# Gram products issued in bursts of their own, and the next chunk's v.r products moved ahead of the state and y products

## The chip, the core and the metric

The kernel runs on one core of one Trainium2 chip. TensorE multiplies into PSUM, ScalarE (ACT) and VectorE (DVE) copy from there to SBUF, GpSimd (POOL) works on SBUF alone, and SP issues most of the transfers. The metric is the device time of one execution in microseconds.

## What is computed

A recurrence over 768 time steps for 4 batches of 8 heads, whose output goes through a routed two-layer network.

```python
for t in range(S):
    y[:, :, t] = np.einsum('bhd,bhde->bhe', rt, state)
    Sa = np.einsum('bhde,bhe->bhd', state, at)
    state_decay = state * wt[:, :, None, :] - np.einsum('bhd,bhe->bhde', Sa, bt)
    state = state_decay + np.einsum('bhd,bhe->bhde', vt, kt)
...
expert_idx = np.argmax(x @ w_gate, axis=1)
h = np.maximum(x_sorted[lo:hi] @ w1[e], 0.0)
y_sorted[lo:hi] = h @ w2[e]
return gate_w[:, None] * y
```

All inputs are f32; S is 768, D is 40, there are 3072 tokens of width 320 and 8 experts with 1024 hidden columns.

## The kernel before, in words

The 768 steps are cut into 12 chunks of 64. A chunk is worked on as two units, each of two batches: 8 groups times 2 halves of the partitions (`HD`), so a product over a unit is 16 matmuls, each of which the trace counts as two passes. The recurrence inside a chunk is turned into matrix products.

For each chunk there are two kinds of work. The *systems* of the next chunk do not need the state: `grams` (products of a and k, b with the decays; the left operand has 128 columns, so these use tiles of another shape than the 64-column products), five `level` products that invert a triangular matrix by halves, `couple` and `whole`. The *rest* of the present chunk needs the state: `right` (ps_q, the right-hand side, first from the state, then from v), `solve` (ps_uT), `zgram` (ps_z), `y_state` and `y_rest` (ps_y), `state` (ps_s), `turned` (ps_S), and `emit` (ps_x), which writes the output rows and gate logits of the chunk before. `atv` (ps_atv, the v.r products) belongs to the next chunk and needs only its inputs.

TensorE, ScalarE and VectorE run in the order in which the code issues their work, and `weave` writes that order: it takes the system pieces of both units by turns (16 pieces a chunk) and puts the matmuls of the rest beside them, two by two, 19 per piece; what doesn't fit beside a piece's 16 matmuls follows it. Items of `rest` that stand in a tuple use all 128 rows of the array; they are not put beside a piece but run as a burst after it, to the end of all such items in a row. `ahead` holds VectorE and GpSimd work (`decay`) for the chunk after next.

A piece's `end` issues the copies out of PSUM. For `grams` these are, per bank pair half, one VectorE multiply (pair, L304) and three ScalarE copies (off L314, nkb L315, GT L316). `parted` is a ScalarE copy of one element (seen, L229) that stands between two products into one bank which use different rows of the array, and TensorE waits for it. PSUM is shared out in two tags with two buffers of two banks each: "sys" for the systems (a unit's Gram products take both) and "rest".

SP issues the loads of the chunk after next in program order; each waits until its buffer's reader is done.

The matmul helper `mm` is line 222, so nearly all of TensorE's rows carry L222 and are told apart by their tiles.

Of the kernel before, what the change touches and what calls it, by code (L numbers as in the profile page):

```python
# [8 lines left out]
F32 = mybir.dt.float32  # L9
# [12 lines left out]
def kernel(  # L22
# [96 lines left out]
    with tc.tile_pool(name="ring", bufs=1) as ring, \  # L119
# [198 lines left out]
            return ts, end  # L318

        def stack(name, s, w):  # L320
            return [sb.tile([128, G, w], F32, name=f"{name}{s}_{par}") for par in range(2)]

        def atv(u):

# [167 lines left out]
        def y_state(us):  # L492
            for u, ps in zip(us, banks("ps_y", T2)):
                c, s = u
                d = units[u]
                d["py"] = ps
                if c:
                    yield [lambda g=g, par=par: mm(
                        ps[own(par), g, :], s_r[s][0][oth(par, D), g, :], d["ri"][oth(par, D), g, :T2],
                        start=(g == 0), stop=False, free=True) for g, par in HD], lambda ps=ps: parted(ps)  # L500

        def y_rest(us):
            for u in us:
                c, s = u
                d = units[u]
                ps = d["py"]

                def end():
                    t = d["y"] = sb.tile([128, G, T2], F32, name="y", bufs=4)
                    nc.scalar.copy(t[:], ps[:])  # L510
                    nc.gpsimd.tensor_tensor(t[:], t[:], d["PT"][:, :, :T2], op=ALU.mult)
                yield [lambda g=g, par=par: mm(
                    ps[own(par), g, :], d["nkb"][par][:, g, :], d["az"][par][:, g, :],
                    start=(c == 0), free=True) for g, par in HD], end
# [22 lines left out]


        def weave(systems, rest, count, ahead, lead=0):
            def flow():  # L540
                for it in rest:
                    alone = isinstance(it, tuple)
                    for ts, end in (it[0] if alone else [it()] if callable(it) else it):
                        for i, t in enumerate(ts):
                            yield t, (end if i == len(ts) - 1 else None), alone

            f = flow()
            kept = []

            def run(n, beside=False):  # L550

                while n > 0:
                    t, end, alone = kept.pop() if kept else next(f, (None, None, None))
                    if t is None:
                        return 0
                    if alone and beside:
                        kept.append((t, end, alone))
                        return n
                    t()
                    if end:  # L560
                        end()
                    n -= 1
                    if alone and n <= 0:
                        n = 1
                        t = next(f, None)
                        if t is not None:
                            kept.append(t)
                        if t is None or not t[2]:
                            n = 0
                return 0  # L570

            ahead = list(ahead)
            per = -(-count // max(len(systems), 1))
            for n, piece in enumerate(systems):
                ts, end = piece()
                left = per
                for i in range(0, len(ts), 2):
                    for t in ts[i : i + 2]:
                        t()
                    left -= min(2, left) - run(min(2, left), True)  # L580
                end()
                run(left)
                if n >= lead and ahead:
                    ahead.pop(0)()
            for a in ahead:
                a()
            run(10 ** 6)

        def chain(u):
            return ([lambda: grams(u)] + [lambda k=k: level(u, k) for k in range(5)]  # L590
                    + [lambda: couple(u), lambda: whole(u)])

        def systems(us):
# [2 lines left out]
        def rest(us, nx, before):  # L596
            last = us[0][0] + 1 == NS
            ps = [right(us), solve(us)] + [lambda u=u: zgram(u) for u in us]
            ps += [y_state(us), (emit(before),)] if before else [y_state(us)]
            if not last:  # L600
                ps += [(state(us),)]
            ps += [(y_rest(us),)] + [lambda u=u: atv(u) for u in nx]
            if not last:
                ps += [turned(us)]
            return ps

        with tc.manual_schedule(engines={mybir.EngineType.PE, mybir.EngineType.DVE, mybir.EngineType.Activation}):
# [21 lines left out]
            def with_fill(piece, n):  # L629
                def f():  # L630
                    ts, end = piece()

                    def end_():
                        end()
                        for _ in range(n):
                            if fill:
                                fill.pop(0)()
                    return ts, end_
                return f
            one[:3] = [with_fill(one[0], 2), with_fill(one[1], 2), with_fill(one[2], 1)]  # L640

            def late(u):
                return [lambda i=i: decay(u)[i]() for i in range(5)]
# [275 lines left out]
```

## Time and profile before

| | us |
|---|---|
| median of 2 runs | 1236.79 (1234.4 to 1239.18) |
| the profiled execution | 1237.3 |
| its span, first to last instruction | 1235.5 |
| TensorE busy in matmuls | 1031.9 (84% of the span) |
| VectorE, ScalarE, GpSimd busy | 365.1, 340.1, 363.0 |
| Gram products (ps_gram), 768 passes | 144.8 |
| level products (ps_lv), 3840 passes | 244.1 |

A busy row of TensorE is not TensorE at its peak: matmuls are pipelined, and one row's duration overlaps the next. How long a stretch takes is read from the starts of its rows in the timeline. The granted clock stands in the windows as a share of 2.4 GHz.

### The profile page before, as it was taken

The numbers are of one execution on the slowest core, as the hardware profiler recorded it, in microseconds if no ns is written. First come the engines' busy times: TensorE is split into PE (matmuls) and PEld (weight loads), VectorE is DVE, ScalarE is ACT, GpSimd is POOL, SyncE is SP. The second block draws the span as 40 slices with busy tenths as digits, with TensorE's granted clock in tenths as the row PEclk, the third lists the DMA queues.
The fourth block names the chain that finished last, engine by engine and source line by source line (L and its number), as shares of the span: only waits on it lengthen the run. The fifth ranks groups of instructions, "written<-read, shape, count | busy, mean of one in ns | idle before, by whom it ended". The sixth has DMA issues, their size and how long they took to land. (4 is left out here: it accounts for less than half of the span.)

```text
span 1235.5 us, 32075 instructions
## 1 busy us (share of the span) xinstructions
PE 1031.9 (84%) x14204; PEld 770.7 (62%) x14204; DVE 365.1 (30%) x681; ACT 340.1 (28%) x732; POOL 363.0 (29%) x393
## 2 busy tenths in 40 slices
PE   1788879788787878787887888785599999999996
PEld 1667768676777767686867777685244554455444
DVE  2623452433414252524424252303311011011100
ACT  0324342433323343424334233432001111011110
POOL 8434342422423243423323342212501211220001
PEclk9966776666757676666667576765599999999998
DMA  3121221111202121111112010003612322231100
GB/s 85 43 46 31 48 48 26 38 36 33 45 22 46 28 51 23 41 32 34 40 32 46 2 24 12 13 3 74 183 54 89 102 79 94 75 121 59 45 16 17
DMA packets 119584, 59.82 MB, mean 48 GB/s; under 512 B 103825, under 2 KB 115091, under 8 KB 119444
## 3 DMA queue, kind: packets, MB, share of 16 engines
q1 hardware_dynamic: 109156, 47.55, 15.0%
q0 software_dynamic: 3072, 9.20, 2.4%
q8 instruction: 113, 1.85, 0.6%
q10 hardware_dynamic: 7216, 1.00, 0.5%
q14 instruction: 27, 0.22, 0.1%
HBM read 49.83 MB, written 9.19 MB: 48 GB/s over the span
## 5 line engine op out<-in xcount | busy, mean ns | idle before, releaser
L222 PE MATMUL ps_lv<-pair,N 64*64 64x96 f32 (+2 forms) x3840 | 244.1, 270 | 43.1 <-DVE pair L373 21.0
L222 PEld LDWEIGHTS ps_lv<-pair,N 64*64 64x64 f32 x3840 | 208.5, 161 | 51.8 <-ACT GT L316 21.8
L823 PE MATMUL hp<-xgT,w 128*128 128x512 f32 (+1 forms) x384 | 192.3, 631 | 0.0
L222 PE MATMUL ps_gram<-ai,kb 40*128 40x104 f32 x768 | 144.8, 441 | 42.1 <-POOL ai L275 24.7
L836 PE MATMUL zp<-w,h_sb 128*128 128x320 f32 x512 | 145.0, 433 | 0.0
L347 DVE STREAM_TRANSPOSE N<-pair 128x512 f32<-128x512 f32 x120 | 83.8, 699 | 193.7 <-ACT pair L370 192.9
L823 PEld LDWEIGHTS hp<-xgT,w 128*128 128x128 f32 (+1 forms) x384 | 63.3, 189 | 123.7 <-issue 122.6
L222 PEld LDWEIGHTS ps_gram<-ai,kb 40*128 40x128 f32 x768 | 97.2, 283 | 61.4 <-POOL ai L275 24.7
L836 PEld LDWEIGHTS zp<-w,h_sb 128*128 128x128 f32 x512 | 94.6, 191 | 34.5 <-issue 0.8
L842 POOL DMA_INDIRECT out_dram<-zo,s_idx x32 | 31.8, 992 | 279.1 <-ACT zo L841 251.2
L304 DVE TENSOR_TENSOR pair<-ps_gram,nup 64x512 f32<-64x512 f32 x48 | 33.1, 689 | 268.6 <-PE ps_gram L222 267.8
L284 POOL TENSOR_TENSOR kb<-kb,wi 128x512 f32<-128x512 f32 x48 | 61.0, 1270 | 118.6 <-DVE wi L281 104.5
L828 DVE TENSOR_SCALAR h_sb<-hp 128x512 f32<-128x512 f32 x32 | 22.1, 692 | 247.5 <-PE hp L823 247.5
L281 DVE RECIPROCAL wi<-PT 128x128 f32<-128x128 f32 x96 | 88.3, 925 | 0.1
L310 POOL TENSOR_TENSOR pair<-pair 128x256 f32<-128x256 f32 x24 | 17.4, 724 | 238.3 <-DVE pair L304 238.3
L830 ACT ACTIVATE h_sb<-hp 128x512 f32<-128x512 f32 x32 | 19.1, 597 | 202.1 <-PE hp L823 196.9
L370 ACT COPY pair<-ps_lv 128x512 f32<-128x512 f32 x96 | 56.1, 584 | 63.2 <-PE ps_lv L222 51.0
L222 PE MATMUL ps_q<-st,ai 40*64 40x40 f32 x704 | 69.9, 291 | 3.3 <-ACT seen L229 3.3
L222 PE MATMUL ps_atv<-ri,v 40*64 40x104 f32 x768 | 71.6, 286 | 0.0
L462 POOL TENSOR_TENSOR az<-az,up 128x512 f32<-128x512 f32 x48 | 59.5, 1271 | 30.2 <-ACT az L461 30.1
L222 PEld LDWEIGHTS ps_q<-st,ai 40*64 40x64 f32 x704 | 47.1, 181 | 29.5 <-issue 20.8
L222 PE MATMUL ps_q<-vu,GT 64*64 64x40 f32 x768 | 55.6, 305 | 7.9 <-ACT q L431 4.6
(163 smaller groups left out, 1434.6 us busy)
## 6 DMA issues: line engine op xcount, KB each, us to landing
w<-in_moe_w_dram SPq DMA_DIRECT2D x8, 1280.0 KB
w<-in_moe_w_dram SPq DMA_DIRECT2D x8, 1024.0 KB
kb<-in_packed_dram SPq DMA_DIRECT2D x176, 40.0 KB
v<-in_packed_dram SPq DMA_DIRECT2D x96, 40.0 KB
wp<-in_packed_dram SPq DMA_DIRECT2D x96, 40.0 KB
ri<-in_packed_dram SPq DMA_DIRECT2D x96, 40.0 KB
x_rows<-xr SPq DMA_DIRECT2D x48, 80.0 KB
a<-in_packed_dram SPq DMA_DIRECT2D x88, 40.0 KB
```

The source lines that it names most:

```text
L222: nc.tensor.matmul(out_, lhsT=lhs, rhs=rhs, start=start, stop=stop, skip_group_check=free)
L281: nc.vector.reciprocal(wi[:, h, p : p + 2], by_batch(d["PT"][:, :, 1:])[:, h, p : p + 2])
L284: nc.gpsimd.tensor_tensor(kb, kb, wi[:, h, :, None, :].to_broadcast([128, NP, 2, T2]), op=ALU.mult)
L304: nc.vector.tensor_tensor(parts(nt)[own(par)], ps[own(par), :, :T2].rearrange("q g (a t) -> q g a t", a=2), nup[own(par)].rearrange("q (a ...
L347: nc.vector.transpose(N[:].rearrange("q g a t -> q a g t"), nt)
L370: nc.scalar.copy(parts(new[:, :2]), ps[:, :, :T2].rearrange("q g (a t) -> q g a t", a=2))
L462: nc.gpsimd.tensor_tensor(t[:], t[:], up64[:, None, :].to_broadcast([128, G, T2]), op=ALU.mult)
L823: nc.tensor.matmul(hp[:, :cols], lhsT=g["w"][0][:dsz, db, fb * 128 : (fb + 1) * 128], rhs=g["xT"][:dsz, db, :cols], start=(db == 0), stop= ...
L828: nc.vector.tensor_relu(g["h"][:, fb, :cols], hp[:, :cols])
L830: nc.scalar.activation(g["h"][:, fb, :cols], hp[:, :cols], AF.Relu)
L836: nc.tensor.matmul(zp[:], lhsT=g["h"][:, fb, j * 128 : (j + 1) * 128], rhs=g["w"][1][:, fb, :], start=(fb == 0), stop=(fb == FB - 1),)
L842: ins_ = nc.gpsimd.indirect_dma_start(out=out[:, :], out_offset=bass.IndirectOffsetOnAxis(ap=g["si"](j), axis=0), in_=zo[:], in_offset=Non ...
```

## The change

Gram pieces are marked in a list, `alone`, and `weave` puts nothing beside them; the 19 matmuls of the rest that belong to such a piece follow its end. The flag that was called `alone` is now `full`. In `rest`, `emit` moves from behind `y_state` to its front and out of the burst with `state` and `y_rest`, the `atv` products come next, and `y_state` moves from ahead of `emit` to behind `state`. So that `atv` can write while the present chunk's vu and az are still read, `stack` gets two buffers.

```diff
@@ -318,7 +318,7 @@
             return ts, end
 
         def stack(name, s, w):
-            return [sb.tile([128, G, w], F32, name=f"{name}{s}_{par}") for par in range(2)]
+            return [sb.tile([128, G, w], F32, name=f"{name}{s}_{par}", bufs=2) for par in range(2)]
 
         def atv(u):
 
@@ -539,10 +539,10 @@
         def weave(systems, rest, count, ahead, lead=0):
             def flow():
                 for it in rest:
-                    alone = isinstance(it, tuple)
-                    for ts, end in (it[0] if alone else [it()] if callable(it) else it):
+                    full = isinstance(it, tuple)
+                    for ts, end in (it[0] if full else [it()] if callable(it) else it):
                         for i, t in enumerate(ts):
-                            yield t, (end if i == len(ts) - 1 else None), alone
+                            yield t, (end if i == len(ts) - 1 else None), full
 
             f = flow()
             kept = []
@@ -550,17 +550,17 @@
             def run(n, beside=False):
 
                 while n > 0:
-                    t, end, alone = kept.pop() if kept else next(f, (None, None, None))
+                    t, end, full = kept.pop() if kept else next(f, (None, None, None))
                     if t is None:
                         return 0
-                    if alone and beside:
-                        kept.append((t, end, alone))
+                    if full and beside:
+                        kept.append((t, end, full))
                         return n
                     t()
                     if end:
                         end()
                     n -= 1
-                    if alone and n <= 0:
+                    if full and n <= 0:
                         n = 1
                         t = next(f, None)
                         if t is not None:
@@ -577,7 +577,8 @@
                 for i in range(0, len(ts), 2):
                     for t in ts[i : i + 2]:
                         t()
-                    left -= min(2, left) - run(min(2, left), True)
+                    if piece not in alone:
+                        left -= min(2, left) - run(min(2, left), True)
                 end()
                 run(left)
                 if n >= lead and ahead:
@@ -586,8 +587,12 @@
                 a()
             run(10 ** 6)
 
+        alone = []
+
         def chain(u):
-            return ([lambda: grams(u)] + [lambda k=k: level(u, k) for k in range(5)]
+            first_piece = lambda: grams(u)
+            alone.append(first_piece)
+            return ([first_piece] + [lambda k=k: level(u, k) for k in range(5)]
                     + [lambda: couple(u), lambda: whole(u)])
 
         def systems(us):
@@ -596,10 +601,12 @@
         def rest(us, nx, before):
             last = us[0][0] + 1 == NS
             ps = [right(us), solve(us)] + [lambda u=u: zgram(u) for u in us]
-            ps += [y_state(us), (emit(before),)] if before else [y_state(us)]
+            if before:
+                ps += [(emit(before),)]
+            ps += [lambda u=u: atv(u) for u in nx]
             if not last:
                 ps += [(state(us),)]
-            ps += [(y_rest(us),)] + [lambda u=u: atv(u) for u in nx]
+            ps += [y_state(us), (y_rest(us),)]
             if not last:
                 ps += [turned(us)]
             return ps
@@ -637,7 +644,8 @@
                                 fill.pop(0)()
                     return ts, end_
                 return f
-            one[:3] = [with_fill(one[0], 2), with_fill(one[1], 2), with_fill(one[2], 1)]
+            alone.append(with_fill(one[0], 2))
+            one[:3] = [alone[-1], with_fill(one[1], 2), with_fill(one[2], 1)]
 
             def late(u):
                 return [lambda i=i: decay(u)[i]() for i in range(5)]
```

On TensorE, at the turn from the first unit's Gram products (ai_1_108) to the second's (ai_1_110), before:

```order
L222 MATMUL ps_gram<-ai_1_108,kb_1_102 128x104 x2
L222 MATMUL ps_q<-st_0_127,ai_0_107 64x40 x2
L222 MATMUL ps_q<-st_0_128,ai_0_109 64x40 x3
L222 MATMUL ps_gram<-ai_1_110,kb_1_104 128x104 x2
L222 MATMUL ps_q<-st_0_128,ai_0_109 64x40 x2
```

and in the changed kernel, from the last product of the chunk before up to the first ps_q product that reads GT:

```order
L222 MATMUL ps_f<-TT_2187,xt_0_118 64x64 x16
L222 MATMUL ps_gram<-ai_1_108,kb_1_102 128x104 x16
L222 MATMUL ps_q<-st_0_127,ai_0_107 64x40 x16
L222 MATMUL ps_q<-st_0_128,ai_0_109 64x40 x3
L222 MATMUL ps_gram<-ai_1_110,kb_1_104 128x104 x16
L222 MATMUL ps_q<-st_0_128,ai_0_109 64x40 x13
L222 MATMUL ps_q<-vu_0_1923,GT_1541 64x40
L222 MATMUL ps_q<-vu_1_1924,GT_1541 64x40
```

The 16 Gram products of a unit stand together, and the 16 + 3 and 13 + 6 ps_q products follow them (the rows show the first two of the six).

On ScalarE, the same place before, the copies out of the first unit's Gram banks with the marker copies (seen) around them:

```order
L229 COPY seen<-ps_q 1x1
L314 ACTIVATE off_0_115<-ps_gram 32x8x32
L315 COPY nkb_0_1_120<-ps_gram 128x8x40
L316 COPY GT_2371<-ps_gram 64x512
L314 ACTIVATE off_0_115<-ps_gram 32x8x32
L315 COPY nkb_0_1_124<-ps_gram 128x8x40
L316 COPY GT_2371<-ps_gram 64x512
L229 COPY seen<-ps_q 1x1
```

and in the changed kernel:

```order
L314 ACTIVATE off_0_115<-ps_gram 32x8x32
L315 COPY nkb_0_1_120<-ps_gram 128x8x40
L316 COPY GT_2353<-ps_gram 64x512
L314 ACTIVATE off_0_115<-ps_gram 32x8x32
L315 COPY nkb_0_1_124<-ps_gram 128x8x40
L316 COPY GT_2353<-ps_gram 64x512
L229 COPY seen<-ps_q 1x1
L314 ACTIVATE off_0_116<-ps_gram 32x8x32
```

The marker of the first unit's ps_q products stood ahead of the six copies and now stands behind them, and the second's likewise.

On ScalarE behind the z products, before, from the second unit's last copies to the output copy (xr) of ps_x:

```order
L461 COPY az_0_2133<-ps_z 64x512
L461 COPY az_1_2134<-ps_z 64x512
L370 COPY pair_2666<-ps_lv 128x8x2x32
L229 COPY seen<-ps_y 1x1
L370 COPY pair_2710<-ps_lv 128x8x2x32
L229 COPY seen<-ps_y 1x1
L370 COPY pair_2749<-ps_lv 128x8x2x32
L526 COPY xr<-ps_x 128x320 x2
```

and in the changed kernel:

```order
L461 COPY az_0_1974<-ps_z 64x512
L461 COPY az_1_1975<-ps_z 64x512
L370 COPY pair_2664<-ps_lv 128x8x2x32
L526 COPY xr<-ps_x 128x320 x2
L334 COPY vu_0_2735<-ps_atv 64x320
L334 COPY vu_1_2736<-ps_atv 64x320
L336 COPY az_0_2737<-ps_atv 64x512
L336 COPY az_1_2738<-ps_atv 64x512
L370 COPY pair_2743<-ps_lv 128x8x2x32
```

The output copies, which the second unit of ps_x waits for by way of the reduction behind them, now follow one level copy and not three; the copies of ps_atv follow them, and y's markers come later.

## Rows read from the trace of the kernel before

**Rows 1.** The page: the span of the profiled execution.

```profile
span 1235.5 us, 32075 instructions
```

**Rows 2.** The page's groups: busy us, mean ns of one pass, idle before.

```profile
L222 PE MATMUL ps_gram<-ai,kb 40*128 40x104 f32 x768 | 144.8, 441 | 42.1 <-POOL ai L275 24.7
```

**Rows 3.** Timeline of TensorE, one chunk: start, duration us, tiles, passes, idle before.

```profile
277.09 0.47 PE L222 MATMUL ps_gram<-ai,kb 40*128 40x104 f32 x2
...
277.85 0.47 PE L222 MATMUL ps_gram<-ai,kb 40*128 40x104 f32 x2 [0.29 <-ACT F L409]
...
281.77 0.76 PE L222 MATMUL ps_gram<-ai,kb 40*128 40x104 f32 x4
...
282.45 0.44 PE L222 MATMUL ps_q<-st,ai 40*64 40x40 f32 x4
...
282.82 0.76 PE L222 MATMUL ps_gram<-ai,kb 40*128 40x104 f32 x4
...
283.87 0.76 PE L222 MATMUL ps_gram<-ai,kb 40*128 40x104 f32 x4
...
285.30 0.65 PE L222 MATMUL ps_q<-st,ai 40*64 40x40 f32 x6 [0.30 <-ACT seen L229]
...
296.67 0.86 PE L222 MATMUL ps_q<-vu,GT 64*64 64x40 f32 x10
...
298.81 0.37 PE L222 MATMUL ps_lv<-pair,N 64*64 64x64 f32 x2 [1.28 <-ACT GT L316]
```

**Rows 4.** The same, TensorE, the last chunk with Gram products.

```profile
754.80 0.47 PE L222 MATMUL ps_gram<-ai,kb 40*128 40x104 f32 x2
...
776.37 0.37 PE L222 MATMUL ps_lv<-pair,N 64*64 64x64 f32 x2 [1.28 <-ACT GT L316]
```

**Rows 5.** Windows: length, busy us (count) by engine, PEclk, DMA share, GB/s.

```profile
278.00:280.00 2.00, 2.00 (x26) 1.56 (x26) 0.00 (x0) 0.00 (x0) 0.00 (x0) 0.98 0.00 0
290.00:292.00 2.00, 2.00 (x18) 1.55 (x16) 0.00 (x0) 0.00 (x0) 0.00 (x0) 0.50 0.00 0
304.00:314.00 10.00, 6.92 (x290) 6.02 (x282) 6.63 (x11) 7.64 (x16) 6.42 (x6) 1.00 0.23 52
```

**Rows 6.** Timeline of TensorE in the prologue.

```profile
25.98 3.32 PE L222 MATMUL ps_gram<-ai,kb 40*128 40x104 f32 x28
...
37.31 2.48 PE L222 MATMUL ps_lv<-pair,N 64*64 64x96 f32 x28
...
55.37 1.35 PE L222 MATMUL ps_lv<-pair,N 64*64 64x96 f32 x28
```

**Rows 7.** Timelines of VectorE and ScalarE behind a unit's Gram products.

```profile
284.66 1.41 DVE L304 TENSOR_TENSOR pair<-ps_gram,nup 64x512 f32<-64x512 f32 x2 [12.25 <-PE ps_gram L222]
...
285.10 0.15 ACT L229 COPY seen<-ps_q 1x1 f32<-1x1 f32 x1 [7.30 <-PE ps_q L222]
...
287.26 0.58 ACT L316 COPY GT<-ps_gram 64x512 f32<-64x512 f32 x1
```

**Rows 8.** Waits of TensorE: us in total, times, longest us.

```profile
PE ps_y L222 <- ACT seen L229: 15.3, 11, 1.5
...
PE ps_x L222 <- DVE lg L527: 12.6, 12, 2.3
...
PE ps_s L222 <- DVE lg L527: 7.5, 10, 0.8
```

**Rows 9.** Timelines of ScalarE and VectorE behind the z products.

```profile
308.74 1.18 ACT L461 COPY az<-ps_z 64x512 f32<-64x512 f32 x2
...
310.82 1.18 ACT L461 COPY az<-ps_z 64x512 f32<-64x512 f32 x2
...
312.02 0.58 ACT L370 COPY pair<-ps_lv 128x512 f32<-128x512 f32 x1
...
313.28 0.39 DVE L373 TENSOR_TENSOR pair<-ps_lv,pair 128x256 f32<-128x256 f32 x1
```

**Rows 10.** Timeline of SP: issue of the v loads.

```profile
332.57 4.45 SPq L257 DMA_DIRECT2D v<-in_packed_dram  x8
```

## The prediction, on record before the run

> **What bounds the kernel now.** I read the span first [rows 1]. The profiled execution took 1237.3 us, 1.8 us of it outside the 1235.5 us span; the median of the runs shown is 1236.8, so a sum made against the profiled time needs no correction that matters. TensorE is busy for most of it (the table above). The change touches nothing of the expert layers that end the program, so everything below concerns the recurrence.
>
> The page's groups show where its products are dear: a pass of a Gram product takes 441 ns on average [rows 2] (the trace counts each f32 product as two passes). The timeline of one chunk shows why [rows 3]. The second Gram pass pair starts at 277.85, the first level product of the next chunk at 298.81, and between them Gram and right-hand-side products alternate two by two: four Gram passes start at 281.77, four q passes at 282.45, the next four Gram passes at 282.82. So eight passes take 1.05 us. The stretch lasts 298.81 - 277.09 = 21.7 us. The last chunk's is 776.37 - 754.80 = 21.6 us [rows 4]; there are eleven such stretches (the first of them, with fewer q products, I count like the others). TensorE hardly waits in it, so this is engine time, and engine time on the path: the levels behind it need the Gram results. The windows show the granted clock: 0.98 of 2.4 GHz at the stretch's start, 0.50, which is 1.2 GHz, in its middle, 1.00 in the ten microseconds behind it [rows 5].
>
> **What the change does to the stretch.** It issues the 32 Gram passes of a unit without anything beside them, and the q passes after them. No instruction is added or removed on TensorE, ScalarE, VectorE or GpSimd. What a burst costs is seen in the prologue: 28 Gram passes in 3.32 us [rows 6], 0.119 us each, so 32 in 3.8 us. The profile prints a clock of 1.00 there, but the same 28 level passes took 2.48 us at 37 us and 1.35 us at 55 us [rows 6], so I read the early rows as the lower level. A q pass alone costs (0.86 - 0.65) / 4 = 0.052 us, from ten passes in 0.86 and six in 0.65 [rows 3]; 32 of them 0.86 + 22 x 0.052 = 2.0 us. Four and four then come to 0.47 + 0.21 = 0.68 us of the 1.05, and the other 0.37 us are two changes between the shapes, 0.18 each.
>
> Now the order of waits. The evacuation of a unit's Gram bank pair is a chain of its own: the last pass ends at 283.87 + 0.76 = 284.63, VectorE starts at 284.66, ScalarE's last copy (second GT) ends at 287.26 + 0.58 = 287.84 [rows 7], 3.2 us. In the new order the marker copy (seen) of the first unit's q products stands behind these six ScalarE copies instead of ahead of them; it takes 0.15 us [rows 7], and with 0.05 for the hand-over TensorE gets its next q product 3.4 us after the Gram burst. The 2.0 us of q passes lie inside that gap, and nothing else is queued on TensorE that may pass; who waits is the second unit's Gram burst, and behind it everything. Worked out at 1.2 GHz:
> - first burst: 0.76 us until the second bank is free (277.85 - 277.09), then 30 passes x 0.119 = 3.6; together 4.3
> - evacuation and marker, covering 32 q passes: 3.4
> - six q passes: 0.65
> - second burst: 3.8
> - evacuation and second marker, covering 26 q passes: 3.4
> - twelve q passes ahead of the first level product: 0.65 + 6 x 0.052 = 0.96
>
> The sum is 16.5 us, a gain of 5.2 of 21.7. The first burst falls where the clock row reads 0.98 today; at half the step it takes 0.76 + 1.8 = 2.6 and the gain is 6.9. Whether the level still stands there when the rest has shifted no row tells. I take 6.2, nearer to the end that the clock row supports. Eleven stretches: 68 us. The two prologue bursts lose one interleaved pair each; I leave that out as under 1 us.
>
> **The reordered tail.** Behind the z products, y's state part, the output products (ps_x), the state and y's rest ran in this order, the last three as one burst; now come ps_x, v.r, state, y's state part, y's rest. Three waits of today go: y's state part on its marker 15.3 us over 11, ps_x on the reduction 12.6 over 12, the state on the reduction 7.5 over 10 [rows 8], 1.4 + 1.05 + 0.75 = 3.2 us a chunk. A new one takes their place. The first unit's ps_x products start where z's first copies end, 308.74 + 1.18 = 309.9, and need some 0.8 (16 x 0.052); the second unit's wait for the reduction of the first. In ScalarE's new order that copy stands behind z's second set, which ends at 310.82 + 1.18 = 312.0, and the level copy to 312.6; VectorE's level work ends at 313.67 [rows 9], and only then comes the reduction. So TensorE stands from 310.8 to 313.7, 2.9 us, and y's marker costs 0.3 later, as q's does now [rows 3]: 3.2 against 3.2. Then the split: one burst of 128-row products became three, four more changes of shape at 0.18, 0.7 us. I take a loss of 0.7 a chunk, 8 us. Bounds: if the new wait is only the 1.05 of today, a gain of 1.1; if the marker's 1.4 stays too, a loss of 2.1.
>
> The Trainium skill speaks against this part: TensorEngine Tiling (Array Packing), Key Properties, says that switching the tiling mode, not just the tile, drains TensorE. The trace agrees that a switch costs, by 0.18 us. If a drain meant a q product's whole 0.44 us [rows 3], four would come to 1.8 us a chunk, and the sum would lose another 12 us.
>
> Hidden at nothing: the second buffers for vu and az cost only SBUF, and let v.r's copies land while the state and y's rest still read the old ones. The v loads are issued once v.r is done, at 332.57 now [rows 10], and then about 15 us sooner; the ri loads, which wait for y's state part, go the other way on SP's queue, with wp and a of the second unit behind them. Their readers come most of a chunk later ((754.80 - 277.09) / 7 = 68 us, [rows 3, 4]), which covers them; without that cover, the eight v issues cost their 4.45 us [rows 10] a chunk.
>
> **Sum.** 1237.3 - 68 + 8 = 1177 us. Ends: 57 - 23 = 34 us of gain gives 1203, 76 + 12 = 88 gives 1149.
>
> **Rivals.**
> - The bursts raise the clock. Dense Gram passes keep 2.4 GHz through the whole stretch: 2.6 + 3.4 + 0.35 + 1.9 + 3.4 + 0.5 = 12.2 us, a gain of 9.5 a chunk, 1141 us. For it: the clock is up at the stretch's start [rows 5]. Against: two gaps of over 1 us each follow the bursts. By the Trainium skill (TensorE: Matmul & The Clock Gate, Part 1) the throttled state is the default and activity releases it; by that rule the gaps speak against the higher level. The trace agrees as far as the waits around 298.81 stand in a stretch at 0.50.
> - The clock falls behind ps_x. The 2.9 us gap comes just ahead of 128 passes of levels and v.r; at (2.48 - 1.35) / 28 = 0.040 us more a pass [rows 6] they lose up to 5.1 us, and 0.4 a chunk is left: 1233 us. Against: an idle piece of similar length stands there today.
> - The change does not do what it says. If the prologue's 3.32 us were taken at the higher level, or the shape were not what makes eight passes last 1.05 us, a Gram pass would cost (1.05 - 0.21) / 4 = 0.21 in a burst too, each burst 6.7, the stretch 22.2, and with the tail's 0.7 the time 1252 us. Against: the pair 2.48 and 1.35.
> - Slower: the sparser stretch keeps the clock at 1.2 GHz in the ten microseconds behind it as well. The window 304 to 314 holds 290 passes at 1.00 with 3.1 us idle [rows 5]; 290 x 0.040 = 11.6, less the 3.1 that the idle time takes up, is 8.5 us a chunk: 1237 + 11 x (8.5 - 6.2 + 0.7) = 1270 us. It decides from 5.5 us lost a chunk, about two thirds of that clock. Against: the level products that would raise the clock are as dense as before.
>
> **Numbers.** Forecast 0.66, higher clock 0.13, clock lost behind ps_x 0.10, no gain in the burst 0.05, slower 0.06. The likeliest time is 1177 us, its own range 1149 to 1203. The range 1138 to 1210 takes in the first two cases and leaves out the other 21 in 100. Two per cent, 25 us, is about what a measurement of this kernel tells from no change: the first two cases are faster by more, 0.79; the clock lost behind ps_x and the burst without gain are within it, 0.15; slower 0.06.
>
> **What would show it.** Right: 32 Gram passes in 2 to 3.8 us; ps_q waiting for the marker some 1.4 us twice a chunk; a stretch of 15 to 16.5 us and chunks near 63 us instead of 68; a wait of ps_x on the reduction near 3 us. Wrong: a Gram pass still above 0.2 us in a burst, a chunk of 68 us with the saved time standing as other waits, or windows at 0.50 where 304 to 314 has 1.00.

## The result, and the profile after

The changed kernel takes 1121.45 us (1120.74 to 1122.15, two runs) against 1236.79; the ratio is 0.907, with an interval of 0.899 to 0.915. The direction was forecast, but the gain is 115 us where 60 were expected, and 1121 lies below the range. In the table of the experiments a time is the median of all executions, and a ratio leaves out slow executions, one of four in e1 and one of four in e8.

The page of the changed kernel shows it in the span and in the Gram group (busy us, mean ns of one pass, idle before), which answer to [rows 1, 2]:

```profile
span 1120.3 us, 32041 instructions
...
L222 PE MATMUL ps_gram<-ai,kb 40*128 40x104 f32 x768 | 79.3, 365 | 29.4 <-POOL ai L275 24.7
```

The busy time of the Gram group fell by 65.5 us. But the chunk says more. From the start of one chunk's Gram products to the next's it takes 58.0 us instead of 68.3, in the mean of the nine chunks behind the first. This timeline of TensorE in the changed kernel is the stretch of [rows 3] (start, duration us, tiles, passes, idle before):

```profile
242.65 0.47 PE L222 MATMUL ps_gram<-ai,kb 40*128 40x104 f32 x2
243.40 2.03 PE L222 MATMUL ps_gram<-ai,kb 40*128 40x104 f32 x30 [0.28 <-ACT F L409]
245.35 1.33 PE L222 MATMUL ps_q<-st,ai 40*64 40x40 f32 x32
248.66 0.64 PE L222 MATMUL ps_q<-st,ai 40*64 40x40 f32 x6 [1.97 <-ACT seen L229]
249.23 3.74 PE L222 MATMUL ps_gram<-ai,kb 40*128 40x104 f32 x32
252.91 1.71 PE L222 MATMUL ps_q<-st,ai 40*64 40x40 f32 x26
256.41 0.55 PE L222 MATMUL ps_q<-vu,GT 64*64 64x40 f32 x6 [1.79 <-ACT seen L229]
256.66 0.37 PE L222 MATMUL ps_lv<-pair,N 64*64 64x64 f32 x2
```

From 242.65 to the first level product at 256.66 are 14.0 us; before it was 21.5 in the mean of the nine. The rest of the chunk, from there to the next Gram product, went from 46.8 to 44.0. So 7.5 us a chunk come from the stretch and 2.8 from the rest, together 93 us in nine chunks. The first chunk that has a Gram stretch went from 65.5 to 52.9, which is 12.6. Behind the start of the last stretch 9.2 us were gained, 7.6 of them in that stretch. With 0.2 us ahead of all this, these are the 115.2 us that the span lost. The expert layers took next to no part.

The waits of TensorE in the changed kernel (us in total, times, longest), beside [rows 8]:

```profile
PE ps_q L222 <- ACT seen L229: 37.6, 22, 2.2
PE ps_x L222 <- DVE lg L527: 31.5, 11, 3.0
PE ps_s L222 <- DVE acc L475: 28.5, 10, 2.9
...
PE ps_y L222 <- ACT seen L229: 8.3, 22, 0.4
```

The waits that were forecast have come: q on its marker, 1.7 us twice a chunk, and ps_x on the reduction, 2.9. One has come that was not forecast: the state products wait 2.85 us for acc, the addition of the first unit's state. With that the tail should have become slower than forecast. It became faster, and the windows at its end show where. Before and after, couple and whole products (ps_y<-D, ps_f), the last pieces of the chunk (length, busy us of TensorE (count), granted clock as a share of 2.4 GHz, DMA share, GB/s); first the kernel before:

```profile
336.00:338.00 2.00, 1.25 (x64) 0.99 0.44 99
338.00:344.00 6.00, 6.00 (x143) 0.50 0.02 4
```

and the changed kernel:

```profile
294.40:301.20 6.80, 5.51 (x227) 1.00 0.04 9
```

Before, the clock stood at 1.2 GHz, and from the first ps_S product to the next Gram product it took 10.2 us in every chunk; now it stands at 2.4 GHz, and it takes 6.2 us in most chunks and 6.8 at most (in the one shown).

The way from the end of z to the first ps_S product took 25.8 us in the mean and takes 26.6 now. This is that way in one chunk, first of the kernel before:

```profile
240.65:266.88 26.23, 20.74 (x414) 0.67 0.19 42
```

and of the changed kernel:

```profile
209.81:236.46 26.65, 18.71 (x421) 0.81 0.23 51
```

TensorE stands idle there for 7.9 us instead of 5.5, but it is busy for 2.0 us less, at a mean granted clock of 0.81 instead of 0.67.

### The profile page after: what moved, and what is told of

It reads as the page before. It is cut to its first block, busy times and chain, and to the rows that moved or that the text cites. A ratio compares the mean times of both kernels' runs of the same rounds, so it can differ in the third digit from the quotient of the medians.

```text
span 1120.3 us, 32041 instructions
## 1 busy us (share of the span) xinstructions
PE 893.8 (80%) x14204; PEld 678.3 (61%) x14204; DVE 370.3 (33%) x681; ACT 338.8 (30%) x732; POOL 362.4 (32%) x393
## 5 line engine op out<-in xcount | busy, mean ns | idle before, releaser
L222 PE MATMUL ps_lv<-pair,N 64*64 64x96 f32 (+2 forms) x3840 | 252.6, 281 | 12.9 <-DVE pair L373 5.4
L222 PEld LDWEIGHTS ps_lv<-pair,N 64*64 64x64 f32 x3840 | 220.1, 168 | 19.3 <-ACT GT L316 5.0
L222 PE MATMUL ps_gram<-ai,kb 40*128 40x104 f32 x768 | 79.3, 365 | 29.4 <-POOL ai L275 24.7
L222 PEld LDWEIGHTS ps_gram<-ai,kb 40*128 40x128 f32 x768 | 71.6, 269 | 33.7 <-POOL ai L275 24.7
L222 PE MATMUL ps_atv<-ri,v 40*64 40x104 f32 x768 | 78.1, 288 | 0.8 <-ACT az L461 0.8
L462 POOL TENSOR_TENSOR az<-az,up 128x512 f32<-128x512 f32 x48 | 59.4, 1266 | 29.6 <-ACT az L461 29.6
L222 PE MATMUL ps_q<-vu,GT 64*64 64x40 f32 x768 | 46.2, 303 | 25.5 <-ACT seen L229 18.2
L222 PEld LDWEIGHTS ps_atv<-ri,v 40*64 40x64 f32 x768 | 62.1, 161 | 1.3 <-ACT az L461 1.0
L275 POOL TENSOR_TENSOR ai<-a,PT 128x512 f32<-128x512 f32 x24 | 28.3, 1179 | 105.8 <-DVE PT L271 99.4
L222 PEld LDWEIGHTS ps_q<-vu,GT 64*64 64x64 f32 x768 | 42.6, 218 | 29.2 <-ACT seen L229 19.8
```

The lines of the kernel that those rows point to most:

```text
L222: nc.tensor.matmul(out_, lhsT=lhs, rhs=rhs, start=start, stop=stop, skip_group_check=free)
L275: nc.gpsimd.tensor_tensor(by_batch(d["ai"][:, :, :T2]), d["a"][:], by_batch(PT[:, :, :T2]), op=ALU.mult,)
L462: nc.gpsimd.tensor_tensor(t[:], t[:], up64[:, None, :].to_broadcast([128, G, T2]), op=ALU.mult)
```

## Experiments

**What had to be told apart.** Theory: two gains that have nothing to do with each other. The bursts remove changes of shape on TensorE. The reorder loses about a microsecond where it was expected to, and gains four at the chunk's end because there the granted clock stays up. Rivals: that the bursts raise the clock of the whole chunk (then the order gains nothing by itself); that the order shortens the end by itself, whatever the clock; and for the clock, that it follows the order of the pieces or how full TensorE is in general, rather than certain waits.

All figures in one table; "stretch" is from the first Gram product to the first level product, "last pieces" from the first ps_S product to the next Gram product, all three as means over the nine chunks behind the first, with the lowest and the highest in brackets where they differ by more than a microsecond:

| kernel | us | ratio to before (interval) | chunk | stretch | last pieces |
|---|---|---|---|---|---|
| before | 1237 | | 68.3 | 21.5 | 10.2 |
| changed | 1121.5 | 0.907 (0.899 to 0.915) | 58.0 | 14.0 | 6.3 |
| e1 bursts only | 1146.1 | 0.924 (0.918 to 0.929) | 61.5 | 13.9 | 10.3 |
| e2 reorder only | 1202.8 | 0.972 (0.968 to 0.976) | 65.2 (63.9 to 68.1) | 21.3 | 6.6 (6.2 to 9.4) |
| e5 groups of eight | 1126.9 | 0.911 (0.906 to 0.917) | 57.5 (55.8 to 58.8) | 14.7 | 6.8 (6.2 to 8.4) |
| e4 y's state part first | 1187.2 | 0.958 (0.954 to 0.963) | 65.5 (60.6 to 67.8) | 14.0 | 8.8 (6.2 to 9.5) |
| e7 bursts, units together | 1077.7 | 0.870 (0.868 to 0.873) | 54.6 (53.8 to 55.6) | 13.9 | 10.2 |
| e9 = e7, filled | 1055.4 | 0.852 (0.850 to 0.854) | 52.3 (51.5 to 53.0) | 14.0 | 7.9 |
| e10 = e1, filled | 1112.8 | 0.900 (0.897 to 0.902) | 57.4 (54.1 to 59.4) | 14.0 | 7.9 |
| e3 changed, units together | 1026.4 | 0.829 (0.826 to 0.833) | 49.3 (48.7 to 51.3) | 14.3 (13.8 to 15.4) | 7.9 |
| e6 changed, marker on VectorE | 1091.5 | 0.879 (0.872 to 0.886) | 54.9 (54.3 to 56.8) | 12.0 | 6.8 (6.2 to 8.2) |
| e8 = e3 and e6 | 1005.8 | 0.813 (0.810 to 0.816) | 47.4 (46.6 to 48.8) | 12.5 (11.9 to 13.5) | 7.9 (7.5 to 8.7) |

### e1 and e2: each half alone

e1 keeps the bursts and puts the parts of `rest` back into the old order:

```diff
-            if before:
-                ps += [(emit(before),)]
-            ps += [lambda u=u: atv(u) for u in nx]
+            ps += [y_state(us), (emit(before),)] if before else [y_state(us)]
             if not last:
                 ps += [(state(us),)]
-            ps += [y_state(us), (y_rest(us),)]
+            ps += [(y_rest(us),)] + [lambda u=u: atv(u) for u in nx]
```

> The Gram bursts alone, with the order of the rest as it was before (y's state part, then output products, state and y's rest as one burst, then the v.r products). Theory A: the bursts shorten each Gram stretch from 21.7 to about 14 us, and the gain of the last pieces of a chunk (S, couple and whole products, 10.3 to 6.2 us) belongs to the reordering, so it is missing here: 1237 less 11 x 7.7 less some 6 for the first chunk, about 1146 us, with windows at 0.50 in the last pieces. Theory B: the last pieces run at the higher clock because the stretch ahead and behind became denser, whatever the order: about 1120 us.

e2 keeps the new order and lets q run beside the Gram products two by two, as before:

```diff
-                    if piece not in alone:
+                    if True:
```

> The reordered rest alone, with the Gram products two by two beside the right-hand-side products as before. Theory A: the last pieces keep their 6.2 us at the higher clock, the stretch stays at 21.7: 1237 less 11 x 2.5, about 1209 us. Theory B: the order by itself gains nothing or loses the 0.7 us a chunk that was forecast: 1237 to 1245 us.

Both came out as theory A had it. The bursts alone give 6.8 us a chunk, the reorder alone 3.1, and together they gave 10.3. In e1 the last pieces still take 10.3 us, so the bursts do not lift the clock there; in e2 they take 6.2 to 6.8 in eight of the nine chunks. (The totals of e1 and e2 add up to 125, some 10 more than the changed kernel gained. That lies behind the chunks: what is left of the recurrence after the last whole products takes 24.4 us in e1, most of it at 2.4 GHz, and 33.7 us in the changed kernel, mostly at 1.2.)

One chunk of e2 ran differently from its neighbours, which is an experiment of its own. The first two windows are that chunk's end, the third is the end of the next chunk:

```profile
260.00:263.00 3.00, 1.88 (x96) 1.00 0.11 22
263.00:269.30 6.30, 6.30 (x143) 0.50 0.02 5
...
330.40:334.40 4.00, 3.72 (x143) 1.00 0.02 4
```

The last 143 recorded passes of either chunk, in the same order: 6.3 us at 1.2 GHz and 4.0 at 2.4, a difference of 2.3. In the chunk that lost them, this row of the timeline stands ahead of the fall, a wait of 0.56 us that the other chunk does not have there (both have one of 0.56 for s just before it):

```profile
262.68 0.19 PE L222 MATMUL ps_y<-D,off 64*64 64x32 f32 x1 [0.56 <-issue]
```

So the order alone does not hold the clock up. It makes the end of the chunk such that it mostly stays up.

### e4: y's state part back ahead of the rest

```diff
-            if before:
-                ps += [(emit(before),)]
+            ps += [y_state(us), (emit(before),)] if before else [y_state(us)]
             ps += [lambda u=u: atv(u) for u in nx]
             if not last:
                 ps += [(state(us),)]
-            ps += [y_state(us), (y_rest(us),)]
+            ps += [(y_rest(us),)]
```

> The changed kernel with the Gram bursts, but y's state part put back ahead of the next chunk's v.r products (order: y's state part, v.r products, sums, state, rest of y). Theory (what stands beside the last levels, and so how full TensorE is at the chunk's end, sets the clock of the last pieces): the last pieces from the first state product to the next Gram burst go back to about 10 us at a granted clock of 0.50 in at least part of the chunks, chunk near 61 us, about 1145 us. Rival (the clock stays up whatever the order of these parts is, and only the place of the v.r products ahead of the state counts): the last pieces stay at 6.2 us and 1.00, about 1121 us.

1187 us, slower than either expectation, so it tells the two apart only in part. Its waits:

```profile
PE ps_atv L222 <- ACT az L336: 21.3, 10, 2.1
PE ps_s L222 <- ACT az L336: 19.7, 10, 2.0
```

Four microseconds a chunk that no other version has. y's bank pair is now held from y's state part to y's rest, so v.r and the state share the one buffer that is left of the tag, and wait for v.r's copies. What can be read is again inside the run: the last pieces took 9.3 to 9.5 us in seven of nine chunks, and 6.2 and 6.8 us in the two others, without any difference in order. Over them the granted clock was 0.50 in a chunk of 67.8 us and 0.90 in one of 60.6.

### e7, e9 and e10: what brings the clock down

e7 is e1 with the products of both units of ps_x, the state and y's rest issued one behind the other, and then both units' copies, instead of product, copy, product, copy:

```diff
+        def both(it):
+            ps = list(it)
+
+            def end():
+                for _, e in ps:
+                    e()
+            yield [t for ts, _ in ps for t in ts], end
...
-                ps += [(state(us),)]
+                ps += [(both(state(us)),)]
```

> The Gram bursts with the old order of the last parts, and the products of both units issued ahead of the first unit's copies in the v.r products, the state and y. Theory (the time of the last pieces follows the granted clock, and the clock follows how full the tail is, not the order): last pieces from the first state product to the next Gram burst near 6.5 us at a granted clock near 1.00, and a time more than 55 us under the 1146 us of the bursts alone. Rival (the order itself keeps the clock down: v.r products last before the next chunk): last pieces stay near 10 us at 0.50, 1090 us or more.

(Where the expectation says v.r products, the edit takes ps_x.) It got faster by 68 us, as the theory asked, but the last pieces stayed at 10.2 us, as the rival asked. A fuller tail in general is not what holds the clock: from z to ps_S it is 0.93 in the mean in e7 and 0.69 in e1, and the last pieces are at 0.67 in both. The timeline of TensorE in e7 shows two waits at the chunk's end:

```profile
495.14 0.46 PE L222 MATMUL ps_S<-i,st 40*64 40x40 f32 x9
496.67 0.25 PE L222 MATMUL ps_lv<-pair,N 64*64 64x32 f32 x2 [1.07 <-DVE pair L373]
...
497.99 0.33 PE L222 MATMUL ps_S<-i,st 40*64 40x40 f32 x2 [0.43 <-ACT s L499]
```

The second unit's last level waits 1.07 us for its pair, and ScalarE and VectorE of e7 show why:

```profile
493.82 1.17 ACT L336 COPY az<-ps_atv 64x512 f32<-64x512 f32 x2
494.89 0.58 ACT L370 COPY pair<-ps_lv 128x512 f32<-128x512 f32 x1
```

```profile
495.50 0.71 DVE L347 STREAM_TRANSPOSE N<-pair 128x512 f32<-128x512 f32 x1 [4.56 <-ACT pair L370]
496.14 0.39 DVE L373 TENSOR_TENSOR pair<-ps_lv,pair 128x256 f32<-128x256 f32 x1
```

In the old order v.r stands beside the last levels, and a unit's v.r has 0.85 + 1.17 = 2.0 us of copies. The level's pair copy queues behind them, VectorE behind that, and TensorE behind VectorE. Is it this wait that costs the clock? e9 and e10 answer by adding work. Six products of 64 x 192 whose results nothing reads go into unused columns of the ps_S bank, ahead of that level:

```diff
+            if k == 4 and s == 1:
+                first_ = ts[0]
+
+                def more():
+                    if gap:
+                        for i in range(6):
+                            qs = own(i % 2)
+                            mm(gap["at"][oth(i % 2), :192], d["off"][qs, 0, :], d["GT"][qs, :3, :].rearrange("q g t -> q (g t)"), free=True)
+                    first_()
+                ts[0] = more
```

> The kernel of the bursts with the old order and both units' products together (1077.7 us; last pieces 10.3 us a chunk at a granted clock of 0.50 after a fall at 497.96 us, 1.3 us behind a wait of 1.07 us of TensorE for the pair of the second unit's last level). Six extra products of 64 x 192, whose results nothing reads, are issued into that wait. Theory (the fall follows the two waits in the tail; the old order has them and the new order does not, and that is what the order is worth): the granted clock stays at 1.00 through the last pieces, which take 6.5 to 7 us, and the kernel with more work is faster by 30 to 40 us, 1038 to 1048 us. Rival (the clock falls there for another reason): last pieces still near 10 us at 0.50, 1078 us, or up to 10 us more for what of the products does not fit the wait.

> The kernel of the bursts alone, with the old order (1146.1 us; last pieces 10.2 us a chunk, granted clock down to 0.50 from 554.8 us on, behind the same wait of 1.07 us), with the same six extra products in that wait. Theory (the waits in the tail bring the clock down, and the order is worth what it takes of them): last pieces 6.5 to 7 us at 1.00, 1106 to 1116 us, which with no part of the reorder is below the changed kernel's 1121. Rival (the order itself): 1146 to 1156 us.

Adding work made both kernels faster: e7 by 22 us, e1 by 33. The timeline of e10, the six products in the place of the wait:

```profile
523.74 0.46 PE L222 MATMUL ps_S<-i,st 40*64 40x40 f32 x9
524.01 1.19 PE L222 MATMUL ps_S<-GT,off 64*64 64x192 f32 x12
525.27 0.25 PE L222 MATMUL ps_lv<-pair,N 64*64 64x32 f32 x2
```

The windows of e1, and then of e10, over the same pieces: the end of v.r, the piece with the wait or its filling, and the last pieces.

```profile
545.90:551.80 5.90, 5.90 (x128) 0.83 0.10 22
551.80:554.70 2.90, 1.42 (x62) 1.00 0.33 76
554.70:562.00 7.30, 7.28 (x168) 0.53 0.02 4
```

```profile
523.60:526.40 2.80, 2.49 (x77) 1.00 0.37 85
526.40:531.60 5.20, 4.62 (x169) 1.00 0.02 4
```

The stretch with the wait is as long as it was, 2.8 against 2.9 us, and busy for 2.49 instead of 1.42. What follows takes 5.2 us at 2.4 GHz instead of 7.3 at 1.2. With that it is shown that this wait takes the clock from the pieces behind it. Two other waits of the place (0.43 us for s, 0.39 for D) stand in e10 and did not cost it. In all nine chunks of e9 and of e10 the last pieces take 7.9 to 8.1 us at 1.00. No run put the six products anywhere else, so it is not shown that they would not keep the clock up from another place too. The size was missed in e9: 1055 where 1038 to 1048 were expected, since the last pieces take 7.9 us and not 6.5 to 7. These 2.3 us in each of nine chunks make up nearly all of its 22. In e10 the last pieces take 7.9 as well, and the time fell where it was expected only because a further 1.7 us a chunk was gained between z and ps_S (26.2 to 24.5). Most of that are two chunks of 54.1 us with some 5 less there: in the first of them the granted clock on that way was 0.92 in the mean, in the chunk behind it 0.73. What brought that about was not tested.

So the 4.0 us that the new order takes from the last pieces of most chunks divide: 10.2 to 7.9, 2.3 us, is the clock, with the place of the wait as long as before. From 7.9 to 6.2, 1.7 us, is first of all the wait of 1.07 itself, which the new order does not have, because v.r's copies are no longer queued ahead of the last level. The remaining 0.6 was not told apart; the waits behind that place are no shorter in the changed kernel (0.56 and 0.31 us against 0.43 and 0.39). The Trainium skill bears on it: TensorE: Matmul & The Clock Gate, in the section on PSUM-queue depth-cycling, tells of another kernel in which frequent short idle times between groups of matmuls made the clock swing between its levels. The trace agrees: here a wait of 1.07 us, once a chunk, goes ahead of the fall.

### e3, e6 and e8: the waits that the change brought

e3 is the changed kernel with both units' products together, by the edit of e7.

> The changed kernel, but the products of both units of ps_x, of the state and of y's rest are issued before the copies of the first unit, so that the second unit's products no longer wait for them (waits of 2.9, 2.85 and 0.77 us a chunk in the changed kernel). Theory: these waits are on the path: v.r then waits some 0.5 us for z's copies, so about 5 of the 6.5 us a chunk are gained, 1121 less 55, about 1066 us. Rival: the copies are what the path needs, and the time comes back as waits of later products: above 1105 us.

1026.4 us, 95 less than the changed kernel where 55 were expected. The waits of ps_x on the reduction and of the state on acc, 2.9 and 2.85 us a chunk, are gone from the list. From the end of z to the first ps_S product a chunk of e3 takes 16.3 us in the mean instead of 26.6. TensorE waits 6.1 us less there (1.9 instead of 8.0), and it is busy 4.3 us less with the same passes, since the granted clock is 1.00 instead of 0.81. The stretch and the last pieces gave 1.9 us of it back (table). So the expectation had the waits about right and left out what they cost through the clock. A window of e3, from ps_x to the next chunk's Gram products, of a kind that seven of the nine chunks have (in the two others the clock falls once more in the last pieces):

```profile
246.90:270.80 23.90, 19.99 (x643) 1.00 0.26 59
```

e6 leaves the units and takes q's marker (y's stays) to VectorE, so that it no longer stands behind the six Gram copies on ScalarE:

```diff
-        def parted(ps):
...
-            nc.scalar.copy(seen[64:65], ps[64:65, G - 1, 0:1])
+        seen_v = ring.tile([128, 1], F32, name="seen_v")
+
+        def parted(ps, onv=False):
...
+            if onv:
+                nc.vector.tensor_copy(seen_v[64:65], ps[64:65, G - 1, 0:1])
+            else:
+                nc.scalar.copy(seen[64:65], ps[64:65, G - 1, 0:1])
...
-                        start=(g == 0), stop=False, free=True) for g, par in HD], lambda ps=ps: parted(ps)
+                        start=(g == 0), stop=False, free=True) for g, par in HD], lambda ps=ps: parted(ps, True)
```

> The changed kernel, with the marker that stands between the two units of q moved from ScalarE, where it queues behind the copies of the Gram burst, to VectorE. Theory (the 1.7 to 2.0 us that q waits for the marker twice a chunk lie on the path): the two waits fall to about 0.5 us each, 1.3 to 1.9 us less a chunk and Gram stretch, 1100 to 1107 us. Rival (the next Gram burst and the first level products wait for the evacuation in any case, so that the wait only moves): 1121 us within 0.5%.

1091.5 us, 30 less; expected were 14 to 21. The wait fell from 37.6 to 15.0 us, about 1 us from each of 22:

```profile
PE ps_q L222 <- DVE seen_v L232: 15.0, 22, 1.2
```

The stretch fell by 2.0, a little over the upper end, and the remainder of the chunk by some 1.1, which no wait of the list accounts for; the mean granted clock went from 0.83 to 0.86.

> Both units' products issued together in the changed kernel's order, and q's marker on VectorE as well. Theory (the two gains are at different places of the chunk and add): 1005 to 1012 us. Rival (the marker's wait only moves to the evacuation): 1026 us within 0.5%.

e8 has both edits and takes 1005.8 us, inside its expectation, 19% below the kernel before and the fastest of all. (The marker gave 30 us in e6 and 21 here, so the two gains add only in part.) It also keeps me from making the rule of e10 too simple. Its windows at the seam of two chunks:

```profile
404.00:405.00 1.00, 0.27 (x8) 0.77 0.00 0
405.00:407.98 2.98, 2.98 (x57) 0.50 0.02 5
407.98:411.00 3.02, 2.73 (x44) 1.00 0.05 12
411.00:412.00 1.00, 1.00 (x30) 0.69 0.43 96
412.00:413.00 1.00, 0.10 (x3) 0.50 0.45 101
```

The first fall comes with a wait; the second, at about 411.4, comes while TensorE is busy, with only 0.29 us idle in the three microseconds ahead of it. What brought that one down stays open.

### e5: how much of a burst is needed

```diff
-                for i in range(0, len(ts), 2):
-                    for t in ts[i : i + 2]:
+                by = 8 if piece in alone else 2
+                for i in range(0, len(ts), by):
+                    for t in ts[i : i + by]:
                         t()
-                    if piece not in alone:
-                        left -= min(2, left) - run(min(2, left), True)
+                    left -= min(by, left) - run(min(by, left), True)
```

> The changed kernel with Gram and right-hand-side products beside each other again, but eight by eight and not two by two: 4 changes of shape and not 16 on each unit's way, and the marker copies stand ahead of the Gram copies as before. Theory, a change of shape costs 0.18 us: the stretch is 21.7 less 2 x 12 x 0.18, about 17.4 us, and the time some 3.4 us a chunk above the changed kernel, about 1158 us. Rival, the burst as such (nothing beside the Gram products) is what pays, by the clock: the stretch stays above 20 us, 1190 us or more.

Neither: 1126.9 us, almost the bursts' time. The timeline of e5:

```profile
258.69 1.08 PE L222 MATMUL ps_q<-st,ai 40*64 40x40 f32 x16
259.70 2.04 PE L222 MATMUL ps_gram<-ai,kb 40*128 40x104 f32 x16
261.67 0.86 PE L222 MATMUL ps_q<-st,ai 40*64 40x40 f32 x10
...
264.12 0.37 PE L222 MATMUL ps_lv<-pair,N 64*64 64x64 f32 x2 [0.43 <-ACT GT L316]
```

Sixteen passes of either kind take 261.67 - 258.69 = 2.98 us at 1.2 GHz. Two by two it was 4 x 1.05 = 4.2 [rows 3]. Six of eight changes of shape less save 1.22 us, 0.20 each: the price was right. The expectation of 1158 failed on the rest of the stretch, which it put at 17.4 us and which takes 14.7. Of these 2.7 us, 0.5 are 24 changes at 0.20 and not 0.18, and 0.85 are the last level's wait for GT, 0.43 instead of 1.28 [rows 3], since more q work is left to cover it. The others were not told apart; the granted clock over the stretch is 0.65 in the mean, and was 0.57 in the kernel before. The markers are issued ahead of the last Gram group's copies and are waited for 0.3 us, as in [rows 3]; in the bursts that wait is 1.7 us, twice a stretch. The Trainium skill's page TensorEngine Tiling (Array Packing), Key Properties, names the cost of such a switch, a drain, but no price; here it is 0.20 us between these two shapes at 1.2 GHz.

## Why the prediction was wrong

**Right: the stretch's mechanism and most of its steps.** A change of shape at 0.18 us measured 0.20 (e5). Step by step against the timeline of the changed kernel: first burst 2.7 us (2.6 with the clock up, 4.3 without), evacuation with the marker 3.3 (3.4), six q passes 0.57 (0.65), second burst 3.7 (3.8), evacuation with the marker 3.5 (3.4). The two ends for the first burst were named, and the clock row [rows 5] pointed to the right one. (That TensorE hardly waits in the old stretch was not so: it waited 3.4 of the 21.5 us. In the new one it waits 4.0, so the gain is engine time all the same.)

**Mis-sized: its last step.** The twelve q passes ahead of the first level product, 0.96 us, took 0.25, as the level products went beside them after six passes. With the first burst at 2.4 GHz that makes 14.0 instead of 14.8, a gain of 7.6 where 6.2 was taken, since I set the sum between its two ends. The first stretch gained 8.5. Sixteen of the 55 us that were missed are here: 10 x 1.4 + 2.3. The last pieces, below, are 35, nine times 3.9. The few that are left are sums of smaller things: the first chunk and the end of the recurrence gained 5 and 2 us more than was taken, and from the first level product to ps_S the nine chunks lost 4 more.

**Wrong: the sum of the tail.** It was put at a loss of 0.7 us a chunk and was a gain of 2.8. The step that failed is a term that the sum does not have: the last pieces, from the first ps_S product on, which gained 3.9. Up to that product the tail lost 0.8 us, close to the 0.7, but that was luck, since two errors stand against each other in it. I listed the waits that the new order removes and looked at ScalarE's queue for the new wait of ps_x, and 2.9 us was exactly right. I did not look in the same way at what v.r's copies delay in their new place. VectorE, ScalarE and TensorE of the changed kernel show it:

```profile
282.78 0.71 DVE L347 STREAM_TRANSPOSE N<-pair 128x512 f32<-128x512 f32 x1 [0.44 <-ACT pair L370]
283.42 0.39 DVE L373 TENSOR_TENSOR pair<-ps_lv,pair 128x256 f32<-128x256 f32 x1
283.73 0.47 DVE L475 TENSOR_TENSOR acc<-ps_s,st 128x320 f32<-128x320 f32 x1
```

```profile
281.10 1.17 ACT L336 COPY az<-ps_atv 64x512 f32<-64x512 f32 x2
282.17 0.58 ACT L370 COPY pair<-ps_lv 128x512 f32<-128x512 f32 x1
```

```profile
284.25 1.94 PE L222 MATMUL ps_s<-vu,nkb 128*64 128x40 f32 x32 [2.85 <-DVE acc L475]
```

v.r's copies, a level's pair, VectorE's transpose, and only then acc: the wait that stood at the last level in the old order went along with v.r and stands at the state now, 2.85 us. I had the state's wait as removed, 0.75. So the waits from z to ps_S did not come to 3.2 against 3.2; they rose by 2.6 us in the mean (5.4 to 8.0). Against that the busy time fell by 1.7, the granted clock there being 0.81 in the mean instead of 0.71, which the sum did not have either. What the four changes of shape cost, 0.7 in the sum, was not measured apart.

The missing term was larger. Nowhere did the sum have a row for the last pieces. I took the clock's level from the stretch [rows 5] and from 304 to 314, and left out 338 to 344, where it stood at 0.50, as at this place in every chunk before. The change takes the 1.07 us wait from ahead of those pieces and with it the fall, 3.9 us a chunk, of which e9 and e10 give 2.3 to the clock. My bounds for the tail, a gain of 1.1 to a loss of 2.1, were made of waits alone.

**The rivals.** "The bursts raise the clock" gave 1141 us, the nearest of the cases, but e1 refutes its mechanism: with bursts alone the second burst still runs at 1.2 GHz and the last pieces take 10.2 us. "The clock falls behind ps_x" came true in its place: windows of the changed kernel show 0.55 in the level and v.r products behind the wait for the reduction and 0.50 in the level and y products behind the wait for acc,

```profile
505.18:508.78 3.60, 3.60 (x50) 0.55 0.32 68
...
518.28:520.78 2.50, 2.50 (x66) 0.50 0.00 0
```

and e3, which removes these waits, has 1.00 there. It was counted as a loss, while the same mechanism gave back more at the chunk's end. (The case without a gain in the burst, put at 1252 us, adds up to 1250; nothing hangs on it.)

**What would show it.** The signs that I named were met in part: Gram bursts of 2.0 to 3.7 us, the marker wait 1.7 instead of 1.4, ps_x 2.9. The stretch (14.0 against 15 to 16.5) and the chunk (58.0 against 63) were better.

## What to carry to other kernels

Before summing a reorder, read the granted clock window by window through the whole period, and ask of each stretch at the lower level which wait stands ahead of it and whether the change moves that wait; e8 shows that this does not find every fall. Where one engine issues copies for two streams in order, a moved piece takes its copies' delay along: follow them to the next reader in the new place. And where products of two units share a tag of buffers, issue both units' products before the first unit's copies; here that was worth 95 us.

## What I had not expected of the hardware

Six products that compute nothing made two kernels 22 and 33 us faster (e9 and e10), by filling a wait of 1.07 us ten times; 2.3 us a chunk of that are shown to be the clock of the pieces behind it. The same 143 passes took 6.3 us at 1.2 GHz in one chunk of e2 and 4.0 at 2.4 in the next, with one more wait of 0.56 us ahead of them. And the second fall of e8, at 411.4 in a busy stretch, has no wait of more than 0.29 us in the three microseconds ahead of it.
